# Another order for a whole program: TensorE's tile kinds grouped, one maximum over partitions moved from GpSimd to VectorE

## The chip, the core and the metric

The kernel runs on one core of a Trainium2 chip. The metric is the device time of one launch in microseconds. A core has TensorE (PE in the profile, its weight loads PEld), VectorE (DVE), ScalarE (ACT), GpSimd (POOL) and SyncE (SP), each with an instruction queue of its own that it works off in order, and 16 DMA engines. The engines meet at semaphores. PSUM, into which TensorE writes, has eight banks.

## The reference, cut to what matters

Attention with a causal window and a linear bias, whose output is the input of a two-layer perceptron. All data are float32.

```python
# q, k, v: (8 batches, 8 heads, 576 rows, 64)
scores = q @ k.T / sqrt(64) + slope[head] * -(abs(i - j))     # kept where 0 <= i - j < 128
attn   = softmax(scores)
x      = (attn @ v), heads joined                             # 4608 x 512
h      = x @ w_in                                             # 512 x 2048
g      = 0.5 * h * (1 + erf(h / sqrt(2)))
out    = g @ w_out                                            # 2048 x 512
```

## The kernel before

Float32 operands are split in two fp16 terms, a high part and a scaled low part, and each product is three fp16 products. Batch 0 and the first token tile of the second layer are done in float32. Of the nine token tiles of 512 rows, the last ones use sums and differences of blocks, seven products in place of eight.

The steps that the prediction names, with their lines:

- `scores` of one batch and one pair of heads: matmuls of 64x64 tiles (`L649`), five PSUM tiles per pair, issued as three pieces of 24, 6 and 24 matmuls. `biased` empties each PSUM tile on VectorE (`L679`) into the buffer `s`; GpSimd sets what the mask excludes (`L684`).
- `softmax`: VectorE's maximum (`L768`), ScalarE's exponential (`L770`), then the division on ScalarE or GpSimd.
- `low_weights`: GpSimd writes the high part of the weights to `e_main` (`L787`, a `TENSOR_SCALAR`), VectorE the low part (`L335`), and a DMA transposes both.
- `weigh`: weights times v, 128x64 tiles (`L831`).
- `mlp_in`: x times w_in, 128x128 tiles (`L880`), three matmuls to a step; `second`: g times w_out (`L929`, in float32 `L926`), 128x128 tiles.
- The scales of w_out: the largest magnitude in each of its blocks of rows is collected in `stwo`, one value per partition and block (`L372` on VectorE, which also prepares the words of w_out with `L382` and `L385`). `scale_out` (the task `zs`) then takes the maximum over the partitions by `over_partitions`, rounds it to powers of two and scales with it. With `early` true that is one GpSimd instruction, `partition_all_reduce` (`L300`), and a `TENSOR_SCALAR` on VectorE (`L301`); with `early` false it is a chain on VectorE (`L305` to `L316`): copy the four quarters of 32 partitions side by side, maximum, 32x32 transposition, maximum, spread, transpose back, and write each quarter.

TensorE thus meets three kinds of tile: 64x64 in scores, 128x64 in `weigh`, 128x128 in the rest.

No scheduler decides the order. `ORDER` is one string of task names, in which each name stands for that task's next step; a loop goes through it and issues each step on its engine's queue. The string `PSUM_BANKS` gives the bank of each PSUM tile in the order in which they are taken, and `TURNS` the copy of each buffer that exists several times:

```python
with tc.manual_schedule(engines=None):
    for step in ORDER.split():
        next(tasks[step])
```

Of the kernel before, what the change touches and what calls it, by code (L numbers as in the profile page):

```python
# [63 lines left out]
n21 t2 e2 t2 e2 t2 t2 p0 n31 W2 a3 e2 n31 l0 j4 F e2 t3 e3 l1 bh l0 e3 i0 t3 t3 l1 w2 e3 W3 i1 H0 H0 j4 i1 e3 w3 l2 j2
p1 j3 p1 lv l2 H2 a5 H3 lv p1 a5 H3 H1 L0 l3 p1 a6 j2 p2 l3 H3 p2 H1 j6 H1 H1 H0 j5 cl H2 p1 H2 i2 H2 f j5 H0 p2 p2 p2
i4 j5 i4 p2 cl lv H8 H8 j3 i5 H9 H8 i5 g0 H9 H8 i2 a7 H9 H10 j3 a6 L3 a7 L2 H3 H9 H4 p3 i3 H10 H4 i3 p3 g3 f p3 lv p3
j7 g1 H5 p3 A0 H5 J0 H11 j7 H10 j6 H10 j6 j7 f A1 p1 i6 i7 i6 J1 i7 lq g8 A0 g9 g2 J0 J0 lq H5 H11 H11 H6 H11 v1 A2 A1
H4 J2 H6 g10 H6 H6 H4 g4 v1 g6 H14 H14 cl A2 H5 J1 H15 v1 g5 bh v1 H12 O H12 H12 H12 v1 J1 f O H7 f H7 H7 p3 q1 q1 H15
H7 H14 H14 J2 u1 H13 q1 q1 q1 H15 q1 q1 u1 q1 H13 lV H13 lV q1 H13 H15 g7 q1 q1 A3 g12 o g11 lV g14 J2 A3 S0 bh g13 B0
J3 o g15 lV B0 J3 B0 A4 B0 S0 J4 p0 B0 S0 B0 v2 B0 o v1 M00 S1 B1 B0 B0 f o J3 B1 o S1 A5 M01 B1 o A4 M01 B1 B1 S2 v1  # L70
S1 M00 O M00 M01 M01 v2 M00 M00 M00 J4 A5 M00 M01 M00 M01 M00 f J4 J5 B1 M10 B1 B1 f M00 A6 M00 O B1 M00 A6 M00 M01 J6
o M11 M01 J5 J6 o O O J6 M10 N00 A7 M11 M10 O A7 v1 M01 M01 M01 M11 o M11 N01 zs lQ N01 o N00 zs M10 M10 M10 M10 J7 S2
M10 zs tl M11 B2 M11 S2 zs M11 N01 N00 v2 B2 J5 B2 O M10 B2 O M10 M10 O M10 B2 O M20 M20 o M10 zs v2 B2 J7 B2 1c S3 B2
lQ J7 M11 B2 M21 M20 M11 N10 M11 M11 M20 S3 M20 N11 zs M20 M20 M20 M20 o M20 zs N11 tl N10 M21 v2 B3 v2 B3 zs v2 B3 v2
M20 B3 B3 S3 o v2 O v2 M30 o B3 o O M20 M21 v2 M21 M20 zs v2 N10 M21 v2 v2 v2 v2 v2 v2 M21 M21 q2 M30 v2 q2 Y0 B3 B3
M30 M30 M30 N11 y0 B3 Y1 1s N20 M31 M21 M21 M21 N20 M21 q2 O M31 N20 M30 q2 N21 y1 N21 M31 M30 M30 M31 q2 q2 q2 M31 q2
N21 o q2 M30 M31 q2 q2 q2 M30 M30 O q2 X1 q2 q2 X1 h0 h0 x0 h0 1c M31 q2 M30 X0 q2 h0 x1 M30 M31 h1 x0 y2 x1 M31 1H4
M31 O k0 k1 N30 M31 x2 1H0 k0 1H3 N30 1H2 N31 k1 q2 h1 1H4 h1 N31 v2 N30 h1 x2 1H2 q2 1H0 h2 X0 q2 N31 k3 1H5 k2 q2
# [1374 lines left out]
```

## Time and profile before

| | |
|---|---|
| time, median of 3 runs | 917.36 us (915.95 to 918.92) |
| profiled execution | 917.64 us |
| its span in the trace | 915.8 us |
| mean granted clock of TensorE | 0.989 |
| TensorE busy | 884.7 us, 97% |
| VectorE busy | 702.2 us, 77% |
| ScalarE busy | 599.0 us, 65% |
| GpSimd busy | 238.5 us, 26% |

Busy times are sums over one profiled execution. Matmuls that follow each other overlap a little in the trace, so the distance from the start of one run of matmuls to the start of the next is the better measure of what a run takes. "Idle before" is the time in which an engine's next instruction had not begun, with the instruction that released it; "issue" means that the trace shows no instruction that it waited for. The granted clock is a share of full speed.

### The profile page before, as it was taken

To read this page: it belongs to the slowest core of one execution; us is meant where nothing else is said; L and a number is where in the kernel's file an instruction comes from. 1 tells how busy PE (TensorE), PEld (TensorE's weight loads), DVE (VectorE), ACT (ScalarE), POOL (GpSimd) and SP (SyncE) were. 2 spreads that over 40 slices of the span, in tenths; PEclk is the share of its full clock that TensorE was granted. 3 is DMA by queue.
4 is the path that set the end of the run, shared out by engine and by line. 5 is a ranking of instruction groups with operands and counts; after the bars stand their busy time and mean duration, and the time that the engine had idled before them with its cause. 6 is when DMAs were issued, how large, how long until landed. Compare 5 with 4: busy or idle time off the path is not lost.

```text
span 915.8 us, 19220 instructions
## 1 busy us (share of the span) xinstructions
PE 884.7 (97%) x7735; PEld 509.4 (56%) x7735; DVE 702.2 (77%) x1229; ACT 599.0 (65%) x1229; POOL 238.5 (26%) x424
## 2 busy tenths in 40 slices
PE   8899968999999999999999899999999999999998
PEld 4644433544445454444544444444554588888887
DVE  6999956798987777657757767868587999866673
ACT  7989956878757764489638382887536644763662
POOL 2110011133314674333324754434600000000000
PEclk9999988999999999999999999999999999999999
DMA  9775652635466423754284178525431001011001
GB/s 302 253 233 175 197 146 52 152 109 150 87 139 164 79 53 76 195 116 122 73 240 117 34 206 183 114 73 118 119 97 38 33 20 51 1 47 48 2 1 47
DMA packets 185129, 102.16 MB, mean 112 GB/s; under 512 B 137424, under 2 KB 166224, under 8 KB 184272
## 3 DMA queue, kind: packets, MB, share of 16 engines
q1 hardware_dynamic: 185040, 100.94, 41.3%
q8 instruction: 60, 0.98, 0.4%
q14 instruction: 29, 0.24, 0.1%
HBM read 51.77 MB, written 14.68 MB: 73 GB/s over the span
## 4 chain that ended last, share of the span: by engine, by line
PE 69%; DVE 7%; POOL 5%; ACT 4%; issue 4%; DMA 1%; DVEq 0%; ACTq 0%; POOLq 0%
PE h L880 23%; PE o L929 17%; PE u_out L1233 5%; PE u L1144 5%; PE av L831 4%; PE v L1144 3%; PE sc L649 3%; PE o L926 2%; ACT s L770 2%; POOL s L779 2%; PE z_out L1233 2%; PE y_out L1233 2%; PE v_out L1233 2%; PE x_out L1233 2%; POOL e_main L787 2%
## 5 line engine op out<-in xcount | busy, mean ns | idle before, releaser
L880 PE MATMUL h<-x,wi 128*128 128x512 f16 x1344 | 307.6, 381 | 3.0 <-ACT g L902 1.5
L880 PEld LDWEIGHTS <-wi 128*128 128x128 f16 x1344 | 126.2, 98 | 155.0 <-issue 7.5
L929 PE MATMUL o<-wo,g 128*128 128x512 f16 x720 | 163.1, 379 | 0.2 <-DVE g L335 0.2
L929 PEld LDWEIGHTS <-g 128*128 128x128 f16 x960 | 91.2, 98 | 109.7 <-DVE g L335 0.7
L770 ACT ACTIVATE s<-s,nmax 128x192 f32<-128x192 f32 x252 | 111.2, 443 | 58.4 <-DVE nmax L768 58.1
L779 POOL TENSOR_SCALAR s<-s,z 128x192 f32<-128x192 f32 x180 | 106.1, 603 | 57.4 <-DVE z L774 22.4
L335 DVE SCALAR_TENSOR_TENSOR e_main<-s,e_main 128x768 f16<-128x768 f32 (+1 forms) x56 | 60.8, 1091 | 36.4 <-POOL e_main L787 36.0
L335 DVE SCALAR_TENSOR_TENSOR g<-g,sg,g 128x512 f16<-128x512 f32 x80 | 66.3, 840 | 24.4 <-POOL g L907 14.4
L902 ACT ACTIVATE g<-h,gs 128x512 f32<-128x512 f32 x80 | 53.4, 684 | 43.5 <-PE h L880 25.8
L679 DVE SCALAR_TENSOR_TENSOR s<-sc,cs,bias_h 128x384 f32<-128x384 f32 x112 | 66.3, 607 | 18.2 <-PE sc L649 17.2
L649 PE MATMUL sc<-kbuf,qbuf 64*64 64x192 f16 (+1 forms) x1656 | 61.9, 260 | 16.8 <-DVE s L679 10.5
L787 POOL TENSOR_SCALAR e_main<-s 128x960 f16<-128x960 f32 (+1 forms) x56 | 59.1, 1058 | 45.6 <-ACT s L777 18.3
L684 POOL MEMSET s<- 64x64 f32 (+1 forms) x112 | 18.7, 171 | 197.5 <-DVE s L679 179.3
L926 PE MATMUL o<-zo,g 128*128 128x512 f32 x128 | 62.3, 633 | 0.3 <-ACT g L896 0.3
L649 PEld LDWEIGHTS <-qbuf 64*64 64x64 f16 x1512 | 34.6, 108 | 47.4 <-issue 45.1
L1233 PEld LDWEIGHTS <-g 128*128 128x128 f16 x576 | 56.4, 98 | 6.9
L768 DVE TENSOR_REDUCE nmax<-s 128x5 f32<-128x960 f32 (+1 forms) x56 | 58.1, 1045 | 2.8 <-POOL s L684 1.7
L907 POOL TENSOR_SCALAR g<-g,sg 128x512 f16<-128x512 f32 x48 | 43.9, 920 | 49.5 <-ACT g L902 49.5
L929 PE MATMUL o<-wo_first,g 128*128 128x512 f16 x240 | 55.0, 379 | 0.0
L831 PEld LDWEIGHTS <-vbuf 128*64 128x64 f16 x1680 | 42.1, 111 | 20.9 <-issue 18.7
L831 PE MATMUL av<-et,vbuf 128*64 128x128 f16 (+1 forms) x1680 | 47.8, 211 | 1.4 <-DVE s L679 1.0
L770 ACT ACTIVATION_READ_ACCUMULATOR s<-s,nmax 128x1 f32 x252 | 47.5, 188 | 0.0
(295 smaller groups left out, 1397.3 us busy)
## 6 DMA issues: line engine op xcount, KB each, us to landing
v<-vp SPq DMA_DIRECT2D x32, 320.0 KB, 4.8
out<-ob SPq DMA_DIRECT2D x33, 256.0 KB, 2.3
raw<-w_in SPq DMA_DIRECT2D x8, 1024.0 KB, 11.4
raw<-w_out SPq DMA_DIRECT2D x8, 1024.0 KB, 5.5
q<-qp SPq DMA_DIRECT2D x7, 1152.0 KB, 7.5
k<-kp SPq DMA_DIRECT2D x7, 1152.0 KB, 7.1
x<-x_all SPq DMA_DIRECT2D x5, 1024.0 KB, 5.2
qbuf<-qp SPq DMA_DIRECT2D x4, 288.0 KB, 6.2
```

What stands on the lines that cost most here:

```text
L335: return nc.vector.scalar_tensor_tensor(out=dst, in0=src, scalar=scale, in1=high, op0=ALU.mult, op1=ALU.subtract)
L649: done = nc.tensor.matmul(ps[bank][o, n, 0:W], a, m, start=(i == 0), stop=(i == len(terms) - 1 and b > 0), skip_group_check=True,)
L679: yield nc.vector.scalar_tensor_tensor(out=s[:, bank[0] : bank[0] + k, :], in0=ps[bank][:, 0:k, 0:W], scalar=cs, in1=bias.broadcast_to([P, ...
L770: yield nc.scalar.activation(s[:, i, :], s[:, i, :], AF.Exp, bias=nmax[:, i : i + 1], accum_out=z[:, i : i + 1])
L779: yield nc.gpsimd.tensor_scalar(s[:, i], s[:, i], z[:, i : i + 1], 1.0, op0=ALU.mult, op1=ALU.mult)
L787: yield nc.gpsimd.tensor_scalar(e[:, r, 0, c], s[:, r], 2.0 ** E_SHIFT, 1.0, op0=ALU.mult, op1=ALU.mult)
L831: done = nc.tensor.matmul(av[r, (j - blocks[0]) * QB : (j - blocks[0] + len(js)) * QB], v32s[b][:, hp, kb, r] if b < EXACT else vbuf[:, vi ...
L880: done = nc.tensor.matmul(ph, wi[n][:, a, cc, k * P : (k + 1) * P], x[:, cc, b, :], start=(i == 0), stop=(i == 3 * NCC - 1),)
L926: done = nc.tensor.matmul(o, g[:, r, c], zo[n][:, n % 2, k * DM : (k + 1) * DM], start=(fc == first), stop=(fc == last))
L929: done = nc.tensor.matmul(o, g[:, r, a, c], wo[n][:, b, k, :], start=(fc == first and i == 0), stop=(fc == last and i == 2),)
L1144: done = nc.tensor.matmul(ps[:, k * HT : (k + 1) * HT], w(a, i)[:, k * P : (k + 1) * P], m(b, i),  start=first and n == 0, stop=True, skip ...
L1233: done = nc.tensor.matmul(self.ps[name][:, tb], f(d, a)[:, k, tb * P : (tb + 1) * P], w(d, b, k), start=first, stop=True, skip_group_check ...
```

## The change

Three tables change, and two lines of code. The order has 3603 steps in place of 3592, the banks and turns are written anew to fit, and `scale_out` calls `over_partitions` with `early` false. The helper's last step uses its argument `floor` in place of the constant `FLOOR`. Of the tables one line stands for the rest:

```diff
 ORDER = """
-8Oy 8Z3 8Lv 8O3 8Z3 8O3 8O3 8Cy 8Lv 8O3 8C3 8Ly 8Ly 8Oz 8Oz 8Lx 8Lx 8Lz 8Lz 8Lz 8Lz
...
+8OU 8OU 8Oy 8Z2 8Ov 8Lv 8Z3 8C2 8Z3 8Lv 8O3 8O3 8O3 8O3 8Cy 8C3 8Oz 8Ly 8Lx 8Lx 8Oz 8Lz 8Ly 8Lz 8Lz 8Lz
 PSUM_BANKS = (
...
-    "425736154027"
+    "570134652071"
...
         for k in range(P // QP):
-            yield nc.vector.tensor_scalar_max(stat[k * QP : (k + 1) * QP, 0:n], back[:, 0:n], FLOOR)
+            yield nc.vector.tensor_scalar_max(stat[k * QP : (k + 1) * QP, 0:n], back[:, 0:n], floor)
...
     def scale_out():
 
-        yield from over_partitions(stwo, NWP, True, STAT_FLOOR)
+        yield from over_partitions(stwo, NWP, False, STAT_FLOOR)
```

What stands in TensorE's queue at the first scores of batch 4, before (`sc4_0_4` is the PSUM tile of batch 4, head pair 0, group 4; `o2_1` and `o2_2` are tiles of the second layer of token tile 2):

```order
L929 LDWEIGHTS g2_2_3682
L929 MATMUL o2_1_4001<-wo4_1847,g2_2_3682 128x512
L649 LDWEIGHTS qbuf_101
L649 MATMUL sc4_0_4_4177<-kbuf_102,qbuf_101 64x192
...
L649 LDWEIGHTS qbuf_101
L649 MATMUL sc4_0_4_4177<-kbuf_102,qbuf_101 64x192
L929 LDWEIGHTS g2_2_3682
L929 MATMUL o2_2_3701<-wo4_1847,g2_2_3682 128x512
```

And there after the change:

```order
L929 LDWEIGHTS g2_0_3589
L929 MATMUL o2_0_4011<-wo_first_2351,g2_0_3589 128x512
L649 LDWEIGHTS qbuf_101
L649 MATMUL sc4_0_4_4026<-kbuf_102,qbuf_101 64x192
...
L649 LDWEIGHTS qbuf_101
L649 MATMUL sc4_0_4_4026<-kbuf_102,qbuf_101 64x192
L649 LDWEIGHTS qbuf_101
L649 MATMUL sc4_0_5_4033<-kbuf_102,qbuf_101 64x192
L649 LDWEIGHTS qbuf_101
L649 MATMUL sc4_0_7_4034<-kbuf_102,qbuf_101 64x192
```

Before, the six matmuls of this piece stand alone between the second layer's tiles; now the next piece of the pair, `sc4_0_5` and `sc4_0_7`, follows them directly.

GpSimd's queue at the scales of w_out, before. `s1_1`, `s1_2` are the buffers `s` of batch 1, head pairs 1 and 2; a bare `ISA` row is an instruction without operands, `ISA stwo` is the reduction over partitions:

```order
L684 MEMSET s1_1_1142 64x64 x2
L787 ISA
L787 TENSOR_SCALAR e_main_105<-s1_0_1055 128x5x192
L787 TENSOR_SCALAR e_main_105<-s1_0_1055 128x4x192
L300 ISA
L300 ISA stwo_96<-stwo_96 128x8
L684 MEMSET s1_2_1326 64x128 x2
L684 MEMSET s1_2_1326 64x64 x2
L787 ISA
L787 TENSOR_SCALAR e_main_105<-s1_1_1142 128x5x192
L787 TENSOR_SCALAR e_main_105<-s1_1_1142 128x4x192
```

After:

```order
L684 MEMSET s1_0_1063 64x64
L684 MEMSET s1_1_1061 64x64
L787 ISA
L787 TENSOR_SCALAR e_main_105<-s1_0_1063 128x4x192
L787 TENSOR_SCALAR e_main_105<-s1_0_1063 128x5x192
L684 MEMSET s1_2_1302 64x128 x2
L787 TENSOR_SCALAR e_main_105<-s1_1_1061 128x5x192
L684 MEMSET s1_2_1302 64x64 x2
L787 TENSOR_SCALAR e_main_105<-s1_1_1061 128x4x192
L684 MEMSET s1_3_1427 64x128 x2
```

The reduction of `stwo` is gone from GpSimd's queue, and with it the two bare `ISA` rows at `L300` and ahead of the third `TENSOR_SCALAR`; the one ahead of the first `TENSOR_SCALAR` stays.

## Rows read from the trace of the kernel before

**Rows 1.** The page's head and its slices: busy us (share) of TensorE, granted clock.

```profile
span 915.8 us, 19220 instructions
...
PE 884.7 (97%) x7735; PEld 509.4 (56%) x7735; DVE 702.2 (77%) x1229; ACT 599.0 (65%) x1229; POOL 238.5 (26%) x424
...
PEclk9999988999999999999999999999999999999999
```

**Rows 2.** TensorE's timeline, 117 to 152 us: start, us, instructions, [idle before <-releaser].

```profile
122.77 0.51 PE L649 MATMUL sc<-kbuf,qbuf 64*64 64x192 f16 x7
130.58 1.17 PE L649 MATMUL sc<-kbuf,qbuf 64*64 64x192 f16 x23 [7.29 <-DVE s L679]
...
144.71 0.27 PE L649 MATMUL sc<-kbuf,qbuf 64*64 64x192 f16 x1
149.44 1.17 PE L649 MATMUL sc<-kbuf,qbuf 64*64 64x192 f16 x23 [4.46 <-DVE square L306]
```

**Rows 3.** VectorE's timeline, 117 to 152 us.

```profile
117.19 1.21 DVE L372 TENSOR_SCALAR_CACHE_REDUCE zo<-zo 128x1024 f32<-128x1024 f32 x1
...
123.34 2.03 DVE L335 SCALAR_TENSOR_TENSOR e_main<-s,e_main 128x768 f16<-128x768 f32 x2 [4.80 <-POOL e_main L787]
129.49 0.17 DVE L301 TENSOR_SCALAR stwo<-stwo 128x8 f32<-128x8 f32 x1 [4.12 <-POOL stwo L300]
...
146.13 0.96 DVE L335 SCALAR_TENSOR_TENSOR e_main<-s,e_main 128x768 f16<-128x768 f32 x1 [6.76 <-POOL e_main L787]
...
148.76 0.62 DVE L679 SCALAR_TENSOR_TENSOR s<-sc,cs,bias_h 128x384 f32<-128x384 f32 x1
```

**Rows 4.** GpSimd's timeline, 99 to 148 us.

```profile
111.74 0.14 POOL L684 MEMSET s<- 64x64 f32 x1 [1.44 <-DVE s L679]
121.52 1.79 POOL L787 TENSOR_SCALAR e_main<-s 128x960 f16<-128x960 f32 x2 [9.63 <-issue]
129.06 0.39 POOL L300 PARTITION_ALL_REDUCE stwo<-stwo  x1 [5.76 <-issue]
...
144.31 1.79 POOL L787 TENSOR_SCALAR e_main<-s 128x960 f16<-128x960 f32 x2 [7.12 <-issue]
```

**Rows 5.** Windows: stretch, length, busy us (instructions) by engine, granted clock of TensorE, DMA share, GB/s.

```profile
23.00:118.00 95.00, 91.53 (x629) 48.32 (x627) 94.18 (x145) 87.48 (x147) 8.66 (x18) 0.98 0.65 217
118.00:257.00 139.00, 125.44 (x1063) 60.90 (x1062) 107.44 (x212) 95.56 (x213) 33.37 (x55) 0.95 0.46 112
...
130.60:134.70 4.10, 4.10 (x27) 2.27 (x27) 3.92 (x11) 1.29 (x4) 0.40 (x2) 0.50 0.79 275
...
149.40:155.20 5.80, 5.76 (x29) 2.90 (x29) 5.47 (x25) 4.53 (x5) 0.97 (x5) 0.50 1.00 205
```

**Rows 6.** TensorE's timeline, 606 to 640 us.

```profile
628.72 0.81 PE L880 MATMUL h<-x,wi 128*128 128x512 f16 x3
629.37 2.75 PE L929 MATMUL o<-wo,g 128*128 128x512 f16 x12
...
635.29 0.69 PE L649 MATMUL sc<-kbuf,qbuf 64*64 64x192 f16 x24
635.91 0.82 PE L880 MATMUL h<-x,wi 128*128 128x512 f16 x3
636.66 0.43 PE L649 MATMUL sc<-kbuf,qbuf 64*64 64x192 f16 x6
637.03 0.82 PE L880 MATMUL h<-x,wi 128*128 128x512 f16 x3
```

**Rows 7.** TensorE's timeline, 262 to 290 us.

```profile
264.11 1.43 PE L649 MATMUL sc<-kbuf,qbuf 64*64 64x192 f16 x54
265.47 0.82 PE L880 MATMUL h<-x,wi 128*128 128x512 f16 x3
```

**Rows 8.** Line L305, the copies of `over_partitions`: ns shortest/median/longest.

```profile
L305 DVE COPY quarters<-stq x24: 147/158/961, 157.0 to 578.6; 32x2 f32<-32x2 f32 x24
```

**Rows 9.** Groups by line: busy us, mean ns of one, idle before.

```profile
L770 ACT ACT_TABLE_LOAD x23 | 29.5, 1283 | 0.4
```

More of the change, by code (lines that the diff above doesn't have):

```diff
@@ L64 @@
[L64 to L78, printed above, removed]
@@ new lines @@
+1g12 1H13 1g9 1H14 1H14 1H14 1H10 1g8 2M00 2M00 2N00 1g11 1H10 2M11 1H10 1g8 1o3 2N00 1g11 2M10 2N01 1H15 1H10 1H15
+1g12 1g11 1g13 1o3 2M10 1o0 2M10 2S2 2S2 1g10 2N01 1g12 1o2 1g14 1H15 2M10 2M11 3Q 2N00 1g14 2B2 2B2 2M11 2N01 2M11
+2M10 2B2 2B2 2B2 2S2 1g14 2M11 2M11 2M11 2M11 1g10 2M11 2M20 2M10 2M11 1s 1g13 3Q 2B2 2B2 1g10 2M10 2M20 2N10 2M20
+2N10 2S3 1o2 1o0 1o2 3Q 2S3 2M20 2M20 2N11 2M20 2M20 2B2 2M20 2N11 2B3 3Q 1g15 2N10 3Q 3Q 2M20 2S3 3V 2B3 2B3 2y0 2B2
+3Q 2M21 3Q 3Q 3Q 3Q 2B3 3Q 3Q 3Q 2N11 3Q 2Y1 3Q 1g15 2B3 2M21 2M20 v2 2B3 2M21 2M20 3Q 3Q 2M20 2Y0 2B3 2y1 2M20 1g15
@@ new lines @@
+1g13 3V 3V 2B3 1o3 3Q 1o2 2M30 2X1 2M21 2M21 2X1 2M21 3Q 2N20 2M21 2B3 1o0 2M30 2M21 2M30 3Q 2x1 2M30 1o0 2M30 2X0
+2M31 2M21 2N20 2x0 2M30 2M21 1o3 3S0 2M31 2M21 2X0 2x1 2N21 2x0 2M30 2M30 2M30 2M30 2M30 2M30 2M31 2M31 2N20 3S0 1k0
+1k2 2N21 3B0 2M31 3B0 3B0 2M30 3B0 1k3 3S1 3S0 2M31 2M31 2N21 3B0 2M31 3B0 2N30 2M31 2M31 2N30 2M31 1o1 2N31 3B0 2N30
+1o1 3B0 2N31 3M00 3B0 3B1 3M01 2H4 3B1 3M01 3M01 2H7 1o1 3B1 2c 3S1 3B1 3S1 2N31 3B1 3B1 2y3 2Y3 3M01 1k2 3M00 2Y2
+3M01 1k3 3M10 3M01 3B1 3M01 3M00 3M00 3M00 2x3 2x3 3M01 3M00 2y2 2X2 3M01 1o1 3B1 2x2 2H1 3s 3M00 1k1 3M01 3B1 2x2 2H7
@@ new lines @@
+5B1 p3 4y3 5M00 5B1 5B0 5B0 5M01 5M01 5B1 5M01 5M01 4X1 5B1 5M01 5M01 5M01 5M01 5M01 5M01 5M00 5M00 5M00 4Y3 4X3 4Y2
+5B1 4y2 3H15 4x1 5M10 4x3 5M00 5M00 3g13 3g14 3H9 4x3 3H9 5M00 3o3 5M11 4X2 3g10 3o3 3H15 6q 5M10 5u 5u 3g13 5M11 3H11
+3H11 3H11 3H11 5M11 4X2 5M11 3H15 3H15 6v 6q 3o2 4x2 4x2 5M11 3H9 6v 3g15 6v 5M01 5N01 5N01 3H9 3g11 4X3 3g11 5M00
+5M11 5M00 5M11 5M11 3g9 5M00 3g11 5M00 5N00 4X2 5S2 5N00 5B2 5B2 3g15 5S2 5B2 5S2 5B2 5B2 3g9 3o1 3g9 5M20 5M11 3g15
+3o1 3o1 3o1 5M20 5M20 5N00 5B2 5B2 5B2 5B2 5M11 5M21 6v 6V 6V 6V 6V 6V 3o2 6V 5N01 6V 5M21 6V 4X3 5M21 5M21 6V 5M10
@@ new lines @@
+6x0 5g0 6N30 5H3 7S1 7S0 4o1 7B0 5g2 7B1 7B1 5H8 7B1 6x1 7B0 4k3 6X0 5H3 5g6 7B0 5H8 6N31 7B0 6X0 7V 7B1 7S1 7B1 7S0
+5g3 4k1 7B0 7S1 7B1 7S0 7B1 7M00 7B0 6Y2 5g3 7B1 7M10 6N30 7M00 6y3 6y2 7B0 7M00 5g3 6x3 5H9 6x2 7B1 7M11 6X0 6x3 5H12
+5H9 5H7 rs 7M00 5H8 7B0 7M00 5H7 7M00 7M00 7B0 7M11 7M00 7M00 7M01 6X2 7M00 7M00 ls 6X1 5g6 7M10 7M11 7M11 ls 7M11
+7M10 5H11 5H7 7M00 7M01 6x2 5g6 6t 7M11 7M00 5H12 7M10 5H9 4k1 5H5 7M01 7M10 5H7 7M01 7M11 5H8 7M11 7M01 7M11 5H12
+7M11 7M11 7M10 5g7 5H1 5g8 7M01 7N00 5H9 5H5 5g9 7M10 7N00 5H1 7M10 7M01 5H1 7M01 5g7 6X2 5g9 5g7 7M01 7M01 7M01 5H5
@@ new lines @@
+7M30 7M21 7M21 7M21 7M21 7M21 7M30 7N21 5g14 5o0 5g14 7M31 7M31 7N20 7M30 5g15 7X0 7M30 7M30 5g12 7M31 5g13 7M30 7X0
+7x1 7N21 7M30 7M30 5g13 7M30 5g13 7N30 5g15 7x1 7N21 7N30 5o3 7N30 5o0 7M31 7X1 7M31 7M31 7M31 5g15 5o0 7x1 7M31 5o1
+7Y2 5k0 7y2 7x2 7N31 7y3 7X0 7N31 7N31 7Y3 rf sa0 5k1 sa0 7x3 sa0 sa0 sa0 6H1 sa0 7x3 7X1 sa0 sa0 sa0 sa0 sa0 sa0 sa0
+6H2 sa0 7X2 6H0 6H1 7x2 6H2 7X1 5o3 sa1 6H7 6H0 6H2 sa1 7X2 sa1 6H4 6H2 6H1 sa1 sa1 6H1 6H0 6H0 sa1 sa1 sa1 sa1 sa1
+sa1 sa1 6g2 6H6 sa1 6g1 sa1 sa2 6H6 6g0 sa2 6g1 sa2 6g1 6H7 sa2 sa2 sa2 sa2 sa2 sa2 sa2 sa2 5o3 6H3 6H3 6H3 6H3 6g3
@@ new lines @@
+6g3 sa3 6g3 6g3 sa2 sa2 sa2 sa3 sa3 7X3 sa3 sa3 sa3 sa3 6g3 sa3 6H7 sa3 7x2 sa3 6H4 6H5 6g3 6g3 7X2 6H6 7X3 7X3 6H4
+sa3 6H4 6H9 6g4 5o3 5k3 6H7 7x3 6g3 6H6 6g6 6H5 sa3 6H5 6g3 6H5 6H14 6H9 6H8 6g7 6g5 6g3 6g7 sa3 6g7 6g7 6H12 6g7 6g7
+6g7 6g3 6g5 6g5 6g7 6g7 6g3 6g7 6H15 6g7 6g7 6H8 sa3 6g7 6H8 6H13 6H13 6g7 6g3 6H13 6g3 6g3 6H9 6H14 6H13 6H12 6H14
+6g7 6H8 6g3 6g7 6H12 5o2 6H9 6H10 6g3 7L 6H10 6g9 6g8 6H11 7i0 6H11 6g9 6g7 6H10 6H10 6H15 7i0 7i0 7i0 7i0 6g9 7i0 7i0
+7i1 6Ov 6H11 7i1 6H11 7i1 7i1 5o2 6g10 7i1 7i1 6H12 6H15 6Ou 6g11 6Oy 6g11 6H14 6g11 6g11 6g11 6g11 6H15 6g11 6g11
@@ L190 @@
+    "4602573102573756215264635241703521437540627545036275034621003462052164251543260153150246371254317062"
+    "570134652071"
 )
@@ L193 @@
     "cx": "0123450123540",
-    "g": "01230123021302130123012301230213012302310",
+    "g": "01230123013201320312031021023012301231203",
     "gs2": "0123",
@@ L197 @@
     "ld": "01010101010101010101",
-    "nmax": "01010101011010101010101010101010",
-    "ob": "012012021021210121021121020212012210101200210201210122101201201202021021021020101210211122120212021020021020121021021202102102",
+    "nmax": "01010101010101010101010110110101",
+    "ob": "012010120212010212021121010120120120212102021021020212020122010120121012020211201012020020110212122101210102121202102120210210",
     "pwq": "0101010",
-    "pwv": "01212121",
-    "pwx": "0120120",
-    "s": "01010101010010101010101010101010110",
+    "pwv": "01212012",
+    "pwx": "0120102",
+    "s": "01010100101010101010101010100101001",
     "scq": "0101010",
-    "scv": "01212120",
+    "scv": "01212121",
     "sg2": "0123",
     "sg8": "01010101",
-    "so": "010101010",
+    "so": "010100101",
     "stq": "0101010",
@@ L211 @@
     "sx": "01201201",
-    "wo": "012301230123",
-    "x": "010101010111010",
-    "z": "01010101011010101010101010101010",
+    "wo": "012323102310",
+    "x": "010010101000101",
+    "z": "01010101010101010101010101001010",
 }
```

208 lines of the change are left out of this document (96 added, 112 removed).

## The prediction

> **What bounds the kernel now.** I read the page's head first. TensorE is busy 884.7 of 915.8 us and its granted clock is at full level in nearly every slice [rows 1], so the time is TensorE's matmuls plus 31.1 us of gaps. That leaves two questions: where the gaps are, and whether TensorE's busy time holds anything besides matmul columns.
>
> The gaps: TensorE's timeline between 120 and 150 us has two large ones, 7.29 us before the scores at 130.58 and 4.46 us before those at 149.44, 11.75 us together [rows 2]. Both runs of scores wait for VectorE to empty an earlier PSUM tile. VectorE's timeline tells why it was late: it stood still for 4.80, 4.12 and 6.76 us, 15.7 us together, each time behind GpSimd [rows 3]. And GpSimd was idle just before the instructions waited for, for 9.63, 5.76 and 7.12 us, with "issue" as the reason [rows 4]. In GpSimd's order a bare `ISA` row stands at each of the three places, wherever the engine goes from `PARTITION_ALL_REDUCE` to `TENSOR_SCALAR` or back. I read it as a change of configuration. So one reduction over partitions, placed between two `low_weights`, makes GpSimd change three times, VectorE queue behind it, and TensorE wait for VectorE. Behind each gap TensorE's granted clock is 0.50, the lower of its two levels, after it had stood still: 4.10 us and 5.76 us of matmuls at half speed [rows 5].
>
> The busy time: between full tiles, a run of score matmuls (64x64 tiles) takes from its start to the next start 0.62 us for 24 matmuls and 0.37 us for 6 [rows 6], and 1.36 us for 54 in one run [rows 7]. The 54 are 24 + 6 + 24, which apart cost 1.61 us: each boundary left out saves 0.125 us. At a run's other end, three `mlp_in` matmuls take 0.65 us when full tiles follow (628.72 to 629.37), and 0.75 us when scores follow (635.91 to 636.66) [rows 6]: 0.10 us. A detour from full tiles to small ones and back costs about 0.22 us, 0.11 us a switch, and no view shows it as a wait.
>
> **The change, part by part.**
>
> *Tile kinds.* The matmuls are the same 7527. Counted in TensorE's order, the kind changes 275 times before and 134 times after. From batch 1 on, the runs of scores go from 72 to 30 and the runs of `weigh` from 48 to 18. 141 switches at 0.11 us are 15.5 us, all of it on TensorE, the engine that sets the end. The bounds: 12 us if the return from a `weigh` run is free, since the 0.125 us is seen on scores alone (42 detours at 0.22 us and 30 at 0.10 us); 17 us if every switch costs 0.12 us. I take 15.5 us, from the two rows that show each direction.
>
> *The reduction.* `scale_out` loses one GpSimd instruction of 0.39 us [rows 4] and the changes around it: of the three in this stretch two go. The first stays, ahead of the first `low_weights`; it took up to 9.63 us [rows 4]. What covers it: in VectorE's order, between the last eviction of pair 1 and the first `e_main`, there are now ten instructions of the kind of `L372` (seven of `L382` and `L385`, three of `L372`), each some 1.2 us [rows 3], 12 us without the small ones; before there were five, 6 us. So GpSimd should be ready 2 us or more before VectorE arrives; if that cover is gone, up to 7.29 us come back. Gained are the two gaps, 11.75 us, and half of the 4.10 + 5.76 us at half clock, 4.9 us: 16.7 us. In exchange VectorE gets the chain over partitions: 13 instructions (4 copies, maximum, transposition, maximum, copy, transposition, 4 maxima), at 0.158 us as the copy of the same helper [rows 8] 2.1 us, less the 0.17 us of the maximum that goes [rows 3]: +1.9 us. They wait for nothing but VectorE's own results. Queued behind them are the evictions of pair 3, for which its scores wait, so the chain costs between nothing and 1.9 us; it is counted in the next term.
>
> *VectorE with less time.* From 118 to 257 us VectorE is busy 107.44 of 139 us [rows 5]. Take away the 16.7 us and some 3 us of switches, add 1.9 us: 109.3 of 119 us, 92%. The nearest row for such a load is 23 to 118 us: VectorE busy 94.18 of 95 us, TensorE still 91.53 us [rows 5]. TensorE lost 3.5 us there, which is 4.4 us on 119. I take 5 us of new waits. The bounds: 12 us, the two gaps back under other names; and −2 us, because a new order may also shorten some of the other 19.4 us of gaps (31.1 − 11.75), of which I count none.
>
> *The rest.* The tables of banks and buffers follow the order. ScalarE's table loads go from 48 to 54, 6 of 1.283 us [rows 9], 7.7 us on an engine that is busy 95.56 of 139 us from 118 to 257 us [rows 5]: hidden by that slack, and part of the upper bound of new waits if it is not. The other floor in the helper's last step is another constant: nothing.
>
> *Sum.* 915.8 − 15.5 − 16.7 + 5 = 888.6 us of span. The profiled execution took 917.64 us, 1.84 us more than its span: 890.4 us. It lies 0.28 us above the median of 917.36 us, so I forecast 890 us.
>
> One thing speaks against long runs of small tiles. To empty one PSUM tile of scores costs VectorE 0.62 us [rows 3], to fill one costs TensorE 0.27 us (1.36 us for five, [rows 7]). The Trainium skill, "TensorEngine Tiling (Array Packing)", PSUM Bottleneck, says that tiling speeds up the matmuls but not the emptying of PSUM, which may then become the bound. By that rule the longer runs lose at their ends what the switches give, as the third rival below works out (927 us); by the rows, whose two waits for evictions both go back to GpSimd, the sum stays at 890 us.
>
> **The rivals.**
>
> *VectorE becomes the bound after 118 us.* The episode's 16.7 us come back as many shorter waits between 118 and 257 us, and only the switches count: 917.4 − 15.5 = 902 us. For it: 92% busy on an engine whose instructions stand in a fixed order. Against it: 99% from 23 to 118 us cost TensorE only 3.5 us [rows 5].
>
> *The switches save nothing.* The 0.125 us could be the last columns of a run draining, which other orders hide as well. Then 917.4 − 16.7 + 5 = 906 us. Against it: the run of 54 has the same neighbours as the shorter ones and still is 0.25 us cheaper than its parts.
>
> *Slower: long runs of scores wait for the evictions.* The longest run grows from 54 matmuls in 5 PSUM tiles to 84 in 8. VectorE needs 5.0 us for 8 tiles, TensorE 2.2 us, so a backlog of 2.8 us stands at the end of a run, in which full tiles must cover and VectorE's other work comes late. There are 30 such runs; the sum gains 32.2 us from switches and episode, so from 1.07 us of waiting in each, more than half of the backlog of the longest less what covers it, the kernel is slower. At half the backlog, 1.4 us, it takes 917.4 − 32.2 + 42 = 927 us. For it: both large gaps of before are waits for just these evictions. Against it: GpSimd caused them, and after a long run come full tiles that need no eviction of scores.
>
> **How the numbers follow.** Forecast 0.77: 890 us, its own range 881 to 900 us (switches 12 to 17 us, new waits −2 to 12 us). First rival 0.11, 902 us; second 0.06, 906 us; a mix of them that ends at no change 0.02; third 0.04, 927 us. The range of 880 to 906 us leaves out the third, the mix, half of the second and the forecast's edges, less than 2 in 10. What can't be told from no change is 0.3%, 2.75 us: faster 0.94, same 0.02, slower 0.04.
>
> **What would show it.** Right: no gap over 2 us on TensorE between 120 and 160 us; no reduction of `stwo` on GpSimd, and one gap by "issue" there instead of three; the granted clock at full level from 125 to 155 us; TensorE's busy time lower by about 20 us, 15.5 from switches and 4.9 from the clock; and 0.125 us less per joined run of scores. Wrong: TensorE's gaps above 25 us in total, most of them behind VectorE between 118 and 257 us (first rival); busy time near 880 us (second); waits for evictions after the long runs along the whole program (third).

## The result and the profile after

The changed kernel takes 892.05 us (median of 4 runs, 890.68 to 892.45) against 916.65 us before on the same chip: ratio 0.9726, 95% interval 0.9703 to 0.9748. Timed again with the experiments, it took 890.81 us against 917.09 us (0.9701, 0.9681 to 0.9721). The forecast was 890 us.

First the page's head of the changed kernel, to be held against [rows 1].

```profile
span 890.7 us, 19239 instructions
...
PE 867.2 (97%) x7735; PEld 514.7 (58%) x7735; DVE 705.5 (79%) x1241; ACT 607.7 (68%) x1235; POOL 233.2 (26%) x423
...
PEclk9999999999999999999999999999999999999999
```

TensorE is busy 17.5 us less with the same 7735 instructions, and its gaps (span less busy) fell from 31.1 to 23.5 us. That the share stays at 97% says only that it is still the engine that sets the time.

Then TensorE's timeline where the two large gaps were [rows 2].

```profile
137.26 0.69 PE L649 MATMUL sc<-kbuf,qbuf 64*64 64x192 f16 x23 [1.10 <-DVE s L679]
```

One gap of 1.10 us is left of 11.75 us: 23 score matmuls wait for VectorE's eviction. VectorE's timeline there, against [rows 3]:

```profile
121.81 2.02 DVE L335 SCALAR_TENSOR_TENSOR e_main<-s,e_main 128x768 f16<-128x768 f32 x2
```

The first low parts of the weights (`L335` at 121.81, two of them) begin with no wait in front; VectorE came to them 3.3 us later than before (121.81 against 118.54 us, when the wait of [rows 3] began); ten of the 1.2 us steps stand ahead in place of five, as the order said. GpSimd, against [rows 4], and the instruction that the order lists as a bare `ISA`, which the trace names (count: ns, first and last start):

```profile
118.01 2.80 POOL L787 TENSOR_SCALAR e_main<-s 128x768 f16<-128x768 f32 x2 [10.70 <-ACT s L777]
...
130.25 0.99 POOL L787 TENSOR_SCALAR e_main<-s 128x960 f16<-128x960 f32 x1 [4.92 <-ACT s L777]
...
132.92 0.85 POOL L787 TENSOR_SCALAR e_main<-s 128x768 f16<-128x768 f32 x1 [0.87 <-ACT s L777]
```

```profile
L787 POOLq MODIFY_POOL_CONFIG  x2: 4/4/4, 107.3 to 107.4; - x2
```

No row has "issue" any more. `MODIFY_POOL_CONFIG` comes in pairs, one pair to a change of configuration. The one pair that is left at this place stands at 107.3 us, 4.6 us earlier than before (111.9 us), because GpSimd's last `MEMSET` ahead of it comes earlier. GpSimd's idle time of 10.70 us behind it ends with ScalarE's division, so the configuration is inside and was over by then: the first high part begins at 118.01 in place of 121.52 us, 3.8 us before VectorE arrives. The next two high parts follow without a pair. No reduction of `stwo` is there. Last the stretch from 118 to 240 us, which answers to 118 to 257 us in [rows 5]; the columns are as there.

```profile
118.00:240.00 122.00, 116.17 (x1047) 59.15 (x1046) 115.73 (x226) 101.02 (x223) 32.17 (x54) 0.99 0.53 137
```

VectorE is busy 115.73 of 122 us there, 95%, and the clock is at 0.99 in place of 0.95.

The sum of the difference in span, 25.1 us: the two gaps 11.75 us; half of the matmuls at half clock behind them 4.9 us; new gaps −4.1 us (31.1 − 11.75 = 19.4 us became 23.5); new half clock −1.7 us, the net of single stretches, of which the longest new gap leaves one at 228 us (below); what is left for the tile kinds is about 14 us, 0.10 us for each of 141 changes of kind.

```profile
228.30:231.70 3.40, 3.36 (x76) 3.39 (x78) 3.36 (x5) 3.04 (x9) 1.08 (x2) 0.50 0.00 0
```

### The profile page after: what moved, and what is told of

Its sections match the earlier page's. It is cut to its first block, busy times and chain, and to the rows that moved or that the text cites. A ratio compares the mean times of both kernels' runs of the same rounds, so it can differ in the third digit from the quotient of the medians.

```text
span 890.7 us, 19239 instructions
## 1 busy us (share of the span) xinstructions
PE 867.2 (97%) x7735; PEld 514.7 (58%) x7735; DVE 705.5 (79%) x1241; ACT 607.7 (68%) x1235; POOL 233.2 (26%) x423
## 4 chain that ended last, share of the span: by engine, by line
PE 61%; DVE 11%; ACT 5%; DMA 3%; POOL 3%; issue 3%; SPq 1%; DVEq 0%; ACTq 0%; POOLq 0%
PE h L880 18%; PE o L929 17%; PE u_out L1233 5%; PE u L1144 5%; PE av L831 4%; PE v L1144 4%; DMA et<-e_main 2%; DVE e_main L335 2%; PE sc L649 2%; PE z_out L1233 2%; PE v_out L1233 2%; PE y_out L1233 2%; PE x_out L1233 2%; DVE s L679 2%; DVE nmax L768 1%
## 5 line engine op out<-in xcount | busy, mean ns | idle before, releaser
L880 PE MATMUL h<-x,wi 128*128 128x512 f16 x1344 | 300.3, 379 | 2.5 <-DVE s L679 1.5
L880 PEld LDWEIGHTS <-wi 128*128 128x128 f16 x1344 | 129.8, 98 | 158.8 <-issue 3.3
L779 POOL TENSOR_SCALAR s<-s,z 128x192 f32<-128x192 f32 x180 | 100.0, 570 | 90.0 <-DVE z L774 39.4
L335 DVE SCALAR_TENSOR_TENSOR g<-g,sg,g 128x512 f16<-128x512 f32 x80 | 64.9, 820 | 28.7 <-ACT g L905 25.0
L335 DVE SCALAR_TENSOR_TENSOR e_main<-s,e_main 128x768 f16<-128x768 f32 (+1 forms) x56 | 61.8, 1112 | 25.9 <-POOL e_main L787 25.5
L787 POOL TENSOR_SCALAR e_main<-s 128x768 f16<-128x768 f32 (+1 forms) x56 | 62.2, 1113 | 62.4 <-ACT s L777 32.7
L679 DVE SCALAR_TENSOR_TENSOR s<-sc,cs,bias_h 128x384 f32<-128x384 f32 x112 | 66.0, 609 | 4.7 <-PE sc L649 3.4
L649 PE MATMUL sc<-kbuf,qbuf 64*64 64x192 f16 (+1 forms) x1656 | 54.5, 257 | 8.1 <-ACT g L902 2.5
L926 PE MATMUL o<-zo,g 128*128 128x512 f32 x128 | 57.0, 598 | 0.0
L831 PE MATMUL av<-et,vbuf 128*64 128x128 f16 (+1 forms) x1680 | 45.3, 216 | 7.4 <-DMA et<-e_main 5.2
L907 POOL TENSOR_SCALAR g<-g,sg 128x512 f16<-128x512 f32 x48 | 39.1, 820 | 45.4 <-ACT g L902 45.0
```

What stands on the lines that cost most here:

```text
L335: return nc.vector.scalar_tensor_tensor(out=dst, in0=src, scalar=scale, in1=high, op0=ALU.mult, op1=ALU.subtract)
L649: done = nc.tensor.matmul(ps[bank][o, n, 0:W], a, m, start=(i == 0), stop=(i == len(terms) - 1 and b > 0), skip_group_check=True,)
L679: yield nc.vector.scalar_tensor_tensor(out=s[:, bank[0] : bank[0] + k, :], in0=ps[bank][:, 0:k, 0:W], scalar=cs, in1=bias.broadcast_to([P, ...
L779: yield nc.gpsimd.tensor_scalar(s[:, i], s[:, i], z[:, i : i + 1], 1.0, op0=ALU.mult, op1=ALU.mult)
L787: yield nc.gpsimd.tensor_scalar(e[:, r, 0, c], s[:, r], 2.0 ** E_SHIFT, 1.0, op0=ALU.mult, op1=ALU.mult)
L831: done = nc.tensor.matmul(av[r, (j - blocks[0]) * QB : (j - blocks[0] + len(js)) * QB], v32s[b][:, hp, kb, r] if b < EXACT else vbuf[:, vi ...
```

## The experiments

All but chain_alone start from the changed kernel. Times are medians, each beside the kernel before on the same chip. Before took 917.06 us beside the first four kernels; 917.09 us beside after_again, split_scores, split_weigh and fill_228; 916.48 us beside fewer_waits and fewer_split; 917.26 us beside gelu_first and fill_again.

### Is it the configuration, the reduction, or the order?

**allreduce_back**: GpSimd's reduction again, in the new order.

```diff
-        yield from over_partitions(stwo, NWP, False, STAT_FLOOR)
+        yield from over_partitions(stwo, NWP, True, STAT_FLOOR)
...
-v2 zs B2 M11 B2 N10 S3 B2 v1 M20 M20 zs M21 M21 N11 zs N11 M20 o zs B3 zs zs zs zs lQ O zs zs o o zs zs zs zs B3
+v2 zs B2 M11 B2 N10 S3 B2 v1 M20 M20 M21 M21 N11 N11 M20 o B3 lQ O o o zs zs B3
```

> The changed kernel with one part undone: the maximum over partitions of w_out's scales is again GpSimd's reduction, at the place of the first step of VectorE's chain, and VectorE's 13 steps are one again. The order of everything else and the tile kinds stay (134 changes of kind). Theory: two more configurations of GpSimd (to the reduction, 5.8 us before, and back, 7.1 us before) delay the next high part of the weights from 133 to about 145 us; VectorE waits some 10 us for it, TensorE some 9 us behind VectorE and 2 us more at half clock, less the 1.9 us of the chain: 892 + 9 = 901 us (897 to 905). Rival, that the new order hides the reduction wherever it is and only the tile kinds count: 890 to 893 us.

Measured: 901.47 us, ratio 0.9832 (0.9810 to 0.9854). GpSimd's timeline and TensorE's in that run:

```profile
135.22 0.40 POOL L300 PARTITION_ALL_REDUCE stwo<-stwo  x1 [5.78 <-issue]
...
142.71 0.83 POOL L787 TENSOR_SCALAR e_main<-s 128x768 f16<-128x768 f32 x1 [6.97 <-issue]
```

```profile
145.32 1.17 PE L649 MATMUL sc<-kbuf,qbuf 64*64 64x192 f16 x23 [10.96 <-DVE s L679]
```

Both changes of configuration are back, 5.78 and 6.97 us, for a reduction of 0.40 us, and TensorE stands 10.96 us. The rival, that the order hides it wherever it is, is out.

**chain_alone**: the kernel before, with VectorE's chain alone.

```diff
-        yield from over_partitions(stwo, NWP, True, STAT_FLOOR)
+        yield from over_partitions(stwo, NWP, False, STAT_FLOOR)
...
-N01 zs lQ N01 o N00 zs M10
+N01 zs lQ N01 o N00 zs zs zs zs zs zs zs zs zs zs zs zs v2 M10
```

> The kernel before with the other part alone: the order of before (275 changes of kind), only the reduction over partitions of w_out's scales is VectorE's chain, in one piece where the result was taken. Theory: the second and third configuration go, the first (9.63 us) stays and is not hidden in this order, so VectorE still waits 4.8 us at 118 us; TensorE's first gap shrinks from 7.3 to about 5 us, the second of 4.5 us goes with its half clock: 917 - 10 = 907 us (903 to 911). Rival, that only the wait for the reduction's result counts (4.12 us on VectorE): 912 to 915 us. Rival, that the episode goes as a whole without the new order: 900 us.

Measured: 909.57 us, ratio 0.9921 (0.9891 to 0.9951). GpSimd and TensorE:

```profile
122.47 1.79 POOL L787 TENSOR_SCALAR e_main<-s 128x960 f16<-128x960 f32 x2 [9.57 <-issue]
```

```profile
129.76 1.17 PE L649 MATMUL sc<-kbuf,qbuf 64*64 64x192 f16 x23 [5.40 <-DVE s L679]
```

The first configuration (9.57 us) still shows as "issue", TensorE's first gap is 5.40 us, the second gap is gone. So the episode was cured by two things: the chain took two configurations away (7.5 us), and the new order covered the third. The new order alone gives 15.6 us (allreduce_back), the chain alone 7.5 us, both together 26.3 us (after_again): 3 us more than the sum. The gaps say where they come from: the reduction costs TensorE 6.35 us of standing still in the old order (11.75 against 5.40 us), where the first configuration holds VectorE up in any case, and 9.86 us in the new one (10.96 against 1.10 us).

**spare_between** and **spare_before**: a reduction that nobody reads, in two places.

```diff
+    spare_stat = pool.tile([P, NWP], F32, name="spare_stat")
+    nc.vector.memset(spare_stat, 0.0)
+    def idle_reduction():
+        yield nc.gpsimd.partition_all_reduce(spare_stat, spare_stat, P, bass_isa.ReduceOp.max)
...
-M10 N10 v2 zs B2 M11
+M10 N10 v2 pr zs B2 M11
```

```diff
-M01 A4 B1 M10 M11
+M01 A4 B1 pr M10 M11
```

> The changed kernel with one more reduction over partitions on GpSimd, of a spare buffer that nobody reads, between the second and third high part of the weights. The work added is 0.39 us on an engine that is idle 74% of the time. Theory, that the configuration is what costs: as with the reduction put back, without the chain's saving: 892 + 11 = 903 us (898 to 907), and VectorE's wait is for the high part behind it. Rival, that VectorE's wait for the reduction's result was what cost: 892 us.

> The same spare reduction, but placed ahead of the one configuration that the changed kernel still has at this place, so that no configuration is added. Theory, that the configuration costs: 892 us, at most 0.5 us more. Rival, that a reduction over partitions on GpSimd costs by itself (the shared memory port, its own span): as much as in the kernel with it between, some 900 us.

Measured: between, 900.79 us (0.9834, 0.9800 to 0.9869); ahead, 889.97 us (0.9713, 0.9681 to 0.9746). GpSimd and TensorE of the first, then GpSimd of the second:

```profile
135.11 0.39 POOL L1322 PARTITION_ALL_REDUCE spare_stat<-spare_stat  x1 [5.90 <-issue]
...
142.40 0.83 POOL L787 TENSOR_SCALAR e_main<-s 128x768 f16<-128x768 f32 x1 [6.76 <-issue]
```

```profile
145.12 1.17 PE L649 MATMUL sc<-kbuf,qbuf 64*64 64x192 f16 x23 [10.99 <-DVE s L679]
```

```profile
104.97 1.22 POOL L1322 PARTITION_ALL_REDUCE spare_stat<-spare_stat  x1
115.70 2.80 POOL L787 TENSOR_SCALAR e_main<-s 128x768 f16<-128x768 f32 x2 [9.51 <-ACT s L777]
```

The same instruction costs about 10 us where it forces two configurations and nothing that the times show where it forces none. VectorE waits for no result of it in either. The places differ as well as the configurations, but the trace tells them apart: from 100 us on, spare_between has three pairs of `MODIFY_POOL_CONFIG`, at 105.3, 129.4 and 135.6 us, and GpSimd's two idle times by "issue" follow the last two; spare_before has one pair, at 106.1 us, as the changed kernel. That settles the cause: the configuration.

### What does a change of tile kind cost?

**after_again** is the changed kernel as the mark of this set.

> The changed kernel once more, as the mark for the other kernels of this set: 892 us.

Measured: 890.81 us.

**split_scores** and **split_weigh**: steps of `mlp_in` moved into the runs of small tiles. Of each one place of the order:

```diff
-3k0 5N20 6B0 6S2 6S0 4g4 6S2 6S0 6B0 4H6
+3k0 5N20 6B0 4H6 6S2 4H4 6S0 4g4 4H6 6S2 4H6 6S0 6B0
```

```diff
-5y1 6V 5Y0 5X0 5y0 5M31 5x1 5M21 5M21 5N21 5N21 3k3 5c 5Y1
+5y1 6V 4H0 5Y0 5X0 4H0 5y0 5M31 5x1 5M21 5M21 5N21 5N21 3k3 5c 4H0 5Y1
```

> The changed kernel with 28 of its steps of mlp_in (three matmuls of 128x128 tiles each) moved by a few places, into the middle of runs of score matmuls: the same matmuls, but 188 changes of kind in place of 134. Nothing else moves. Theory, that a change of kind costs 0.11 us on TensorE whatever waits: 54 x 0.11 = 5.9 us more, 898 us (896.5 to 899.5), with TensorE's idle time as it was. Rival, that the switches cost nothing and the grouping helps only by what it does to the waits: 892 us. Rival, that long runs of scores cost waits for VectorE's evictions: under 892 us.

> The same for the runs of weigh (128x64 tiles): 17 steps of mlp_in moved into them, 168 changes of kind in place of 134. Theory: 34 x 0.11 = 3.7 us more if the return from 128x64 tiles costs as much as from scores, 1.6 us if only the way out costs; the start-to-start times of the run ends in the trace tell the two apart. Rival, no cost: 892 us.

Measured: 893.57 us (0.9740, 0.9719 to 0.9761) and 893.09 us (0.9730, 0.9714 to 0.9747), 2.8 and 2.3 us over the mark, where 5.9 and 3.7 were expected. The rows say why. First the same runs in TensorE's timeline, whole in the changed kernel:

```profile
462.69 3.00 PE L831 MATMUL av<-et,vbuf 128*64 128x128 f16 x132
465.63 5.35 PE L880 MATMUL h<-x,wi 128*128 128x512 f16 x24
...
476.74 2.17 PE L649 MATMUL sc<-kbuf,qbuf 64*64 64x192 f16 x84
478.85 1.47 PE L880 MATMUL h<-x,wi 128*128 128x512 f16 x6
```

split_weigh has the same 132 matmuls of the first run in four pieces; split_scores has the second run's pieces of 24 and 6 apart:

```profile
460.34 0.55 PE L831 MATMUL av<-et,vbuf 128*64 128x128 f16 x18
460.82 0.82 PE L880 MATMUL h<-x,wi 128*128 128x512 f16 x3
461.57 1.24 PE L831 MATMUL av<-et,vbuf 128*64 128x64 f16 x48
462.74 0.82 PE L880 MATMUL h<-x,wi 128*128 128x512 f16 x3
463.49 0.55 PE L831 MATMUL av<-et,vbuf 128*64 128x128 f16 x18
```

```profile
475.31 0.69 PE L649 MATMUL sc<-kbuf,qbuf 64*64 64x192 f16 x24
475.93 0.82 PE L880 MATMUL h<-x,wi 128*128 128x512 f16 x3
476.68 0.43 PE L649 MATMUL sc<-kbuf,qbuf 64*64 64x192 f16 x6
477.05 0.82 PE L880 MATMUL h<-x,wi 128*128 128x512 f16 x3
```

From start to next start, 132 `weigh` matmuls take 2.94 us whole; in pieces 0.48 + 1.17 us and the same again (the rows from 463.49 on repeat), 3.30 us, 0.12 us for each of three boundaries. The 84 score matmuls (three pieces of 24, two of 6) take 2.11 us whole, and 3 x 0.62 + 2 x 0.37 = 2.60 us apart, 0.12 us each. The three `mlp_in` matmuls between take 0.75 us each time, as in [rows 6]. So a detour costs 0.22 us, from `weigh` as from scores. Then the windows from the end of the float32 products to the last matmul, with the same 6570 matmuls, in the order after_again, split_scores, split_weigh:

```profile
156.90:886.50 729.60, 715.84 (x6570) 435.25 (x6568) 561.19 (x974) 475.00 (x946) 206.54 (x373) 1.00 0.39 94
```

```profile
153.00:888.00 735.00, 724.55 (x6570) 434.99 (x6568) 561.57 (x974) 475.06 (x947) 205.00 (x373) 0.99 0.38 94
```

```profile
153.20:887.10 733.90, 719.44 (x6570) 435.05 (x6568) 562.83 (x974) 475.44 (x946) 204.24 (x373) 1.00 0.39 94
```

TensorE's busy time grew by 8.7 and 3.6 us for 54 and 34 changes of kind. Half clock is in these numbers too: behind 157 us after_again and split_weigh have one stretch of it each, 3.41 us of matmuls, and split_scores has one like it and this one, 6.37 us:

```profile
312.18:319.00 6.82, 6.37 (x134) 5.24 (x135) 6.82 (x15) 2.59 (x5) 6.19 (x11) 0.50 0.80 229
```

Less half of those 6.37 us, 8.7 us become 5.5 us, and the two kernels give 0.10 and 0.11 us a change. In split_scores TensorE's idle time fell from 13.8 to 10.5 us: the moved steps filled waits, so its median understates a change of kind. In split_weigh it did not fall (13.8 to 14.5 us); the window is 4.3 us longer, and what the median lacks of that is the start. The float32 products end between 152.9 and 156.9 us with the same order up to there, which is why the windows begin behind them. The largest part of these 4 us is TensorE's clock, at half early in some executions and not in others; in that of after_again, the last to end them:

```profile
21.77:28.60 6.83, 6.33 (x38) 3.99 (x38) 4.92 (x10) 4.26 (x19) 0.78 (x2) 0.50 1.02 280
```

**fewer_split**, on fewer_waits (below), which has less waiting to fill, moves 42 such steps, 82 changes of kind.

> The same kernel with the steps of mlp_in moved into the runs of scores and of weigh, 42 in all: 218 changes of kind in place of 136, on a program with less waiting that a moved step could fill. Theory, 0.11 us a change: 82 x 0.11 = 9.0 us over fewer_waits. Rival, that the two split kernels were right to show only 0.06 us a change (2.8 and 2.3 us for 54 and 34): 4.9 us.

Measured: 893.26 us (0.9742, 0.9725 to 0.9758) over 889.43 us: 3.8 us, below either theory. Windows of fewer_waits and fewer_split, and the half clock of fewer_split:

```profile
156.10:885.00 728.90, 715.96 (x6570) 435.24 (x6568) 561.82 (x974) 475.03 (x946) 206.48 (x373) 1.00 0.39 94
```

```profile
154.30:888.50 734.20, 725.79 (x6570) 433.06 (x6568) 560.58 (x974) 475.54 (x946) 204.72 (x373) 1.00 0.39 94
310.85:317.68 6.83, 6.11 (x143) 5.38 (x144) 6.83 (x15) 1.82 (x3) 6.10 (x13) 0.50 0.86 222
```

Busy time grew by 9.8 us, of which 1.3 us are half clock (6.11 us of matmuls in place of 3.41 us in fewer_waits), so 8.5 us or 0.10 us a change; idle time fell by 4.5 us, from 12.9 to 8.4 us. The price of a change is settled by the pieces and the busy time: 0.12 and 0.10 us for the two ends of a detour, 0.11 us on average, by the one, 0.10 to 0.11 us by the other. The time of the whole hides more than half of it here, because the moved steps filled waits and the profiled start of fewer_split is 1.8 us shorter.

### The new waits: capacity or order?

**fill_228**: one step of the second layer ahead of the weigh step that waits.

```diff
-2N11 3Q 2Y1 3Q
+2N11 3Q 1o3 2Y1 3Q
...
-3V 3V 2B3 1o3 3Q 1o2
+3V 3V 2B3 3Q 1o2
```

> The changed kernel's longest new wait is 3.7 us of TensorE at 228 us, for the transposed weights of pair 1 of batch 2, and the clock is at half for 3.4 us behind it. Here one step of the second layer (12 matmuls of token tile 1, whose operands are ready) is moved from behind those three weigh steps to ahead of the one that waits. Theory, that TensorE is the bound there and only lacks work: 2.7 us of idle and 1.7 us of half clock go, less 0.2 us for two more changes of kind: 888 us. Rival, that VectorE is the bound in this stretch: the wait comes back within the next 20 us, 892 us.

Measured: 886.44 us (0.9659, 0.9642 to 0.9676), 4.4 us under the mark on the same chip. TensorE's timeline of the changed kernel, then of fill_228:

```profile
228.34 3.62 PE L831 MATMUL av<-et,vbuf 128*64 128x128 f16 x78 [3.69 <-DMA et<-e_main]
```

```profile
222.36 2.76 PE L929 MATMUL o<-wo,g 128*128 128x512 f16 x12
225.59 2.08 PE L831 MATMUL av<-et,vbuf 128*64 128x128 f16 x78 [0.47 <-DMA et<-e_main]
...
241.26 2.75 PE L929 MATMUL o<-wo_first,g 128*128 128x512 f16 x12 [0.90 <-DVE s L679]
```

Of 3.69 us 0.47 are left and 0.90 us come up later. The half clock behind the wait is gone. There TensorE had work that was ready, only in the wrong place. The 4.4 us are more than the repair is worth: the profiled start of fill_228 has no half clock and ends 4.0 us earlier than that of after_again, and from there to the last matmul fill_228 takes 727.1 us (727.3 us in fill_again) against 729.6 us, a gain of 2.5 us. It is the fastest version here.

**fill_again** is the same kernel on another chip, as the mark for gelu_first.

> fill_228 once more, as the mark for gelu_first on the same chip, and to see whether its 886.4 us stand on another chip: 886 us (885 to 888).

Measured: 886.07 us (0.9663, 0.9643 to 0.9684). It stands.

**fewer_waits**: fill_228 and two repairs more, at 271 and at 314 us.

```diff
-3N00 3N01 3M11 3N00 2H1 3M11 3M11 2g4 2X3 2H7
+3N00 3N01 3M11 2X3 3N00 2H1 3M11 3M11 2g4 2H7
...
-3M20 3N20 3M30 2g12 2g12 2g14 4Q 2H10 2g14 3N21 3X0 4Q 4S0 3N20 2g12 2g11 2g14 2g13
+2g12 2g14 3M20 3N20 3M30 2g12 2g14 4Q 2H10 3N21 3X0 4Q 4S0 2g12 2g14 3N20 2g11 2g13
```

> The changed kernel with three repairs of the order, on the three longest waits that it has after 200 us: the step of the second layer ahead of the waiting weigh step at 228 us (as in fill_228), VectorE's low part of x for pair 3 ahead of a low part of the weights for which it queues (1.8 us of TensorE at 271 us), and two GELU tiles of token tile 2 ahead of softmax divisions and low parts on GpSimd and VectorE (3.0 us at 314 to 317 us with 3.4 us at half clock behind). 136 changes of kind. Theory, that TensorE is the bound and these are waits of order: 891 - 4.4 - 1.8 - 3.0 - 1.7 = 880 us (878 to 884). Rival, that VectorE is the bound from 118 to 320 us: no better than fill_228, 886 us.

Measured: 889.43 us (0.9697, 0.9676 to 0.9719), 9 us short of the theory and not better than fill_228. Part of that is the start (its float32 products end at 156.1 us, those of fill_228 at 152.9 us), but from there to the last matmul it takes 728.9 us against 727.1 us, and these 1.8 us are one stretch at half clock that the execution of fill_228 lacks (3.41 us from 314.6 us on; that of fill_again has one at 311 us). TensorE's waits at these places in fewer_waits:

```profile
268.56 15.05 PE L880 MATMUL h<-x,wi 128*128 128x512 f16 x69 [1.55 <-DVE s L679]
...
310.44 0.43 PE L649 MATMUL sc<-kbuf,qbuf 64*64 64x192 f16 x6 [0.95 <-ACT g L902]
312.61 0.69 PE L649 MATMUL sc<-kbuf,qbuf 64*64 64x192 f16 x24 [1.73 <-DVE s L679]
314.06 1.38 PE L649 MATMUL sc<-kbuf,qbuf 64*64 64x192 f16 x24 [0.76 <-ACT g L902]
```

In the changed kernel they were 1.77 us before 270.82 and, around 314 to 317 us, 1.96, 0.47 and 0.57 us. The first became 1.55 us at 268.56, the 3.0 us of the others 3.4 us. The second repair was not what its words said: the names moved ahead stood for ScalarE's steps of the two tiles, so GpSimd's queue stayed as it was and only VectorE's order changed.

**gelu_first** does that repair as it was meant, on fill_228.

```diff
-3M20 3N20 3M30 2g12 2g12 2g14 4Q 2H10 2g14 3N21 3X0 4Q 4S0 3N20 2g12 2g11 2g14 2g13
+2g12 2g14 2g12 2g14 3M20 3N20 3M30 4Q 2H10 3N21 3X0 4Q 4S0 2g12 2g14 3N20 2g11 2g13
```

> fill_228 with one repair more, at 314 us. In fewer_waits the names that were moved stood for ScalarE's steps of the two GELU tiles, so GpSimd's queue stayed as it was; here GpSimd's steps of the two tiles stand ahead of the softmax division, the high part and the next division, and VectorE's low parts of the tiles ahead of the low part of the weights. Theory, that the three waits of 3.0 us are GpSimd's order: GpSimd has the tiles 2.3 us earlier, about 1 us of waiting for VectorE's eviction stays, and the half clock of 3.4 us behind them goes: fill_228 less 2 to 3.7 us. Rival, that the feeding engines are short of time there and the waits return as in fewer_waits: as fill_228, within 1 us.

Measured: 887.98 us (0.9675, 0.9658 to 0.9693) against 886.07 us of fill_again, no gain. TensorE in fill_again, then in gelu_first:

```profile
308.96 0.44 PE L649 MATMUL sc<-kbuf,qbuf 64*64 64x192 f16 x6 [1.95 <-ACT g L902]
...
312.76 3.79 PE L831 MATMUL av<-et,vbuf 128*64 128x64 f16 x132
```

```profile
307.03 0.44 PE L649 MATMUL sc<-kbuf,qbuf 64*64 64x192 f16 x6
309.05 0.69 PE L649 MATMUL sc<-kbuf,qbuf 64*64 64x192 f16 x24 [1.58 <-DVE s L679]
311.13 0.32 PE L649 MATMUL sc<-kbuf,qbuf 64*64 64x192 f16 x1 [1.39 <-ACT g L902]
...
312.74 4.99 PE L831 MATMUL av<-et,vbuf 128*64 128x64 f16 x132
```

Between the two rows of fill_again lie the other two waits, 0.47 and 0.57 us. The first wait, 1.95 us, is gone as meant: the six matmuls run at 307.03 in place of 308.96. But VectorE's eviction and a GELU tile come later for it, 1.58 and 1.39 us are new, and the weigh run behind begins at 312.74 as against 312.76 us. There the wait came back with both repairs that were tried, as the first rival said for a longer stretch. That VectorE is short of time there is not shown: from 260 to 320 us of fill_again it is busy 51.09 of 60 us, 85%, against 95% from 118 to 240 us of the changed kernel, where the repair held. Why it returns stays open.

## Why the prediction was right

*The tile kinds* (15.5 us forecast, all of it on TensorE): right in mechanism and size. The balance leaves about 14 us, the price is 0.11 us by the pieces of runs, and 0.10 to 0.11 us by busy time, less the half clock, in split_scores, split_weigh and fewer_split. The trace counts 7735 instructions on TensorE in both kernels, not 7527; the sum does not use that number. The bound of 12 us, the free return from `weigh`, was needless: 0.12 us there too. The second rival, that switches save nothing, is out.

*The reduction* (16.7 us): right. The gaps and the half clock are gone, and spare_between and spare_before show that it was the configuration. One sentence of it goes too far: the reduction forces two of the three changes, and the first is there without it (9.57 us in chain_alone). The cover held, but only half of it is what the prediction named. VectorE came 3.3 us later, and GpSimd also began 3.5 us earlier, which the prediction did not count. chain_alone shows that without the new order the first change still costs a 5.4 us gap. The chain was forecast at 13 x 0.158 us; its four copies take 0.16 to 0.19 us, and the one gap left, 1.10 us, stands where it is interleaved with the evictions of pair 3.

*New waits* (5 us): measured 4.1 us of gaps and 1.7 us of clock. The size held, the reason only in part. The prediction put it down to VectorE at 92% between 118 and 257 us; VectorE is at 95% there, but the largest wait, 3.69 us for transposed weights, was one of order, as fill_228 shows. What does behave as the first rival said, a wait that returns when it is removed, lies between 260 and 320 us (fewer_waits, gelu_first). So the size of this term is in part luck: it was worked out from VectorE's load, and its longest piece had another cause.

Most signs named ahead came out: no gap over 2 us between 120 and 160 us, the clock at full level there, busy time lower by 17.5 us where about 20 were said (1.7 us of the difference are new half clock, the rest is the price of a change). Not one gap by "issue" is left on GpSimd there, where one was said. The third rival, waits for evictions behind the long score runs, is out: in the whole changed kernel TensorE waits 3.8 us for them (`L679`), four times, where it asked for 42 us; behind the run of 84 at 476.74 it goes on with `mlp_in` at once. The bound named by the Trainium skill in "TensorEngine Tiling (Array Packing)", PSUM Bottleneck, did not come to bear here.

## What to carry to other kernels

On an engine that is 97% busy, ask what the busy time is made of: a run's length from its start to the next start, in pieces and whole, shows a price that no wait shows. A rare instruction on a side engine is priced by what the engine must do before and after it, and the row that tells is the idle time with no releaser. And a moved step has two effects, the one it is moved for and the gap that it fills; busy and idle time tell them apart where the total can't.
